# Last mode group summed in PSUM and copied in halves: one change to a fused attention and spectral-mix kernel

## The chip, the core and the metric

The kernel runs on one core of one Trainium2 chip. The metric is the device time of one execution in microseconds (us); the kernel before took 444.08 us in the median of 3 runs (444.06 to 444.13). Engines are called as in the profile: PE is TensorE (PEld its weight loads), DVE is VectorE, ACT is ScalarE, POOL is GpSimd, SP is SyncE, whose queue issues DMAs.

## What is computed

A linear attention with exponential features (batch 8, 8 heads, 576 positions, head size 64) gives x of shape 8 x 576 x 512. Then a spectral mix follows, cut here to what matters:

```
X = rfft(x, axis=1)[:, :64]                    # 64 modes
Yr = X.real @ w_r[m] - X.imag @ w_i[m]         # per mode m, 512 x 512 weights
Yi = X.real @ w_i[m] + X.imag @ w_r[m]
y = irfft(Y, n=576)                            # 64 modes, the rest zero
u = x + y
out = u + maximum(u @ w_ch, 0)                 # w_ch is 512 x 512
```

The mode weights w_r and w_i are the bulk of what is read: 64 x 512 x 512 float32 each. The DMA casts them to bf16.

## The kernel before

**Stages.** The first stage (attention, forward transform, and the early groups of the mode products) ends near 315 us. The second stage works off the remaining mode groups as their weights arrive. The last stage computes the output in 18 units. Inside `tc.manual_schedule()` each engine runs its instructions in the order of the program text, so a place in the text is a place in every engine's queue.

**Mode groups.** There are 32 groups (`groups`). The weights of a group are two tiles, `wr` and `wi`, of 128 x 8 x 512 bf16, each filled by two DMAs of POOL's queue. From group 8 on, a group covers 8 modes and 128 of the 512 input channels, and the passes over the channels add up in `Yacc` (float32, SBUF). `mode_mm` (L415) does the products of a group, 8 with `wr` and 8 with `wi`, each with 32 stationary columns and 512 moving ones, into one PSUM bank `psY`. `mode_sum` (L448) adds `psY` to `Yacc`. In the last pass it writes a bf16 tile `yst` instead (L469); for the last group, 31, in two halves of 256 columns. Group 30's sum goes to `zy7[:, 1]`.

**From a group's sum to Z and Y.** `transposed` (L852) transposes the sum on PE (L855) and copies it to `sY` (L856). From `sY` come Z, its product with w_ch (`whole_z`, L772, for groups 30 and 31), and Y regrouped by batch. They go to `zy` (`zall` and `yall`): one slot per batch, the modes on the partitions. Batch 0 has slot 8, all others their own number.

**x W.** In the waiting time, PE also does x times w_ch ahead: `flip_x` (L696) transposes two tiles of x, and `times_w` (L707) multiplies them in 8 products into two `psW` banks, each copied to `xw` by ACT (L714).

**Output units.** Unit n adds, in PSUM, x W (`add_xw`, L793) and the inverse transform of Z (`add_z`, L801) in `psB`; ACT takes the relu (L806). x (`add_x`, L808) and the inverse transform of Y (`spec`, L815) go to `psA`; DVE adds the relu to it (L820). Eight of the 18 units are "late": they skip `add_x`, and POOL adds x afterwards (L823). SP issues the output DMAs (L953). Even units use the PSUM bank pairs T0 (`psB`) and T1 (`psA`) of the pool `psumA`; odd units use T2 and T3, which lie in a pool that is opened at n = 1, when `psumL` (tags `tr`, `pW` with two banks, `pY`) is closed. So unit 1's `psB` waits until all of `psumL` is free.

**The order at the seam** (L905 to L937). After group 30: one `times_w`; the `wr` half of group 31; the last `times_w`, with ACT's copy of group 30's Z (`z7`, in T1) to `zy7` between its two `xw` copies; two SP DMAs of `zy7` to `zy`; `add_xw` of unit 0; the `wi` half of group 31 (which waits for the last weights); `add_x` of unit 0; the sum in two halves by DVE, each sent to `yall` by a DMA; transposes, copies, Z of group 31 (L925), its rows of Y (`psR`, L927), the copies to slot 8 (L929, L930), the copy `st` of the whole Z (L932), and DMAs from `st` to the other slots. Then the units start.

Of the kernel before, what the change touches and what calls it, by code (L numbers as in the profile page):

```python
# [26 lines left out]
def kernel(  # L27
# [420 lines left out]
    def mode_sum(k, psY, pb=None):  # L448
        g, gi = groups[k]
        if gi < 0:  # L450
            G = -1 - gi
            if g == 0:
                nc.vector.tensor_copy(Yacc[:, 2 * G:2 * G + 2, :], psY)  # L453
            else:
                nc.vector.tensor_tensor(
                    out=Yacc[:, 2 * G:2 * G + 2, :], in0=psY, in1=Yacc[:, 2 * G:2 * G + 2, :],
                    op=ALU.add)
        elif g < 3:
            nc.vector.tensor_tensor(
                out=Yacc[:, gi, :], in0=psY, in1=Yacc[:, gi, :], op=ALU.add)  # L460
        else:

            cuts = [0, DMODEL] if k < 31 else [0, DMODEL // 2, DMODEL]
            yst = []
            for a, b in zip(cuts, cuts[1:]):
                t = zy7[:, 1] if k == 30 else pb.tile(
                    [128, b - a], BF16, name="yst", tag="yst" if k < 31 else f"yst{a}",
                    bufs=2 if k < 31 else 1)
                nc.vector.tensor_tensor(out=t, in0=psY[:, a:b], in1=Yacc[:, gi, a:b], op=ALU.add)  # L469
                yst += [t[:, x:x + 128] for x in range(0, b - a, 128)]  # L470
                Yst.append((t, gi, a, b))
            return yst

# [203 lines left out]
    psumA = ctx.enter_context(tc.tile_pool(name="psumA", bufs=1, space=bass.MemoryType.PSUM))  # L679
    psum_cm = tc.tile_pool(name="psumL", bufs=1, space=bass.MemoryType.PSUM)  # L680
    psum = psum_cm.__enter__()

    zy = pb.tile([128, B_ + 1, 2, DMODEL], BF16, name="zy", bufs=1)
    zall, yall = zy[:, :, 0], zy[:, :, 1]
    zy7 = pb.tile([128, 2, DMODEL], BF16, name="zy7", bufs=1)
    Yst = []
    xw = pb.tile([128, B_ * NCH - N_EARLY, DMODEL], BF16, name="xw", bufs=1)

    todo = list(range(N_EARLY, B_ * NCH, 2))
# [3 lines left out]
    def slot(b):  # L693
        return b or B_
# [12 lines left out]
    def times_w(between=None):  # L707
        i, sT = ahead.pop(0)
        for x in range(2):
            ps = psum.tile([128, DMODEL], F32, name="psW", tag="pW", bufs=2)  # L710
            for dc in range(4):
                nc.tensor.matmul(ps, lhsT=sT[:, x, dc, :], rhs=wchb[:, dc, :],  # L712
                                 start=(dc == 0), stop=(dc == 3))
            nc.scalar.copy(xw[:, i + x - N_EARLY, :], ps)  # L714
            if x == 0 and between:
                between()
# [73 lines left out]
    def cuts(u):  # L790
        return (slice(0, 1), slice(1, 2)) if u["cut"] else (slice(0, 2),)

    def add_xw(u):  # L793
        u["psB"] = ps = u["pool"]().tile([128, 2, DMODEL], F32, name="psB", tag=u["tags"][0])
        for r, x, b, c, idn, ci in parts(u):
            i = b * NCH + c
            nc.tensor.matmul(ps[r, x, :], lhsT=idn,  # L797
                             rhs=xw0[:, i, :] if i < N_EARLY else xw[:, i - N_EARLY, :],
                             start=True, stop=False)

# [5 lines left out]
            nc.scalar.activation(u["o"][:, s, :], ps[:, s, :], ACT.Relu)  # L806

    def add_x(u):  # L808
        u["psA"] = ps = u["pool"]().tile([128, 2, DMODEL], F32, name="psA", tag=u["tags"][1])
        if not u["late"]:  # L810
            for r, x, b, c, idn, ci in parts(u):
                nc.tensor.matmul(ps[r, x, :], lhsT=idn, rhs=xs_all[:, b * NCH + c, :],
                                 start=True, stop=False)
# [13 lines left out]
    for n, (b, c, late) in enumerate(seq):  # L827
        u = dict(b=b, c=c, late=late == 1, half=c == 4, cut=n in (0, 17), n=n,
                 tags=("T0", "T1") if n % 2 == 0 else ("T2", "T3"),
                 pool=(lambda: psumA) if n % 2 == 0 else (lambda: psum))  # L830
        units.append(u)

    def output_tile(u):
# [15 lines left out]
                        ap=[[9 * DMODEL, 64], [5 * DMODEL, 2], [1, m * DMODEL]]),  # L849
                o[:, s, :].rearrange("p c e -> p (c e)")))  # L850

    def transposed(yst, sY, gi, pts, ident):  # L852
        for (a, b), pt in pts:
            for dc in range(a, b):
                nc.tensor.transpose(pt[:, dc - a, :], yst[dc], ident)  # L855
            nc.vector.tensor_copy(sY[:, a:b, gi % 2, :], pt)  # L856

    def modes_of(k, part, psY=None):
        if part == 0:
            while issue["k"] < min(k + NW, 32):  # L860
                weights(issue["k"])
                issue["k"] += 1
            issue_weights()
        return mode_mm(k, "pY", (part,), psY)

    def piece():
        times_w()
# [1 line left out]
            flip_x()  # L869

    ident_q = pb.tile([128, 128], BF16, name="ident_q", bufs=1)
    issue = dict(k=k_in)
    pieces_behind = (22, 24, 26, 28, 30)
    with tc.manual_schedule():
        flip_x()
        flip_x()
        nc.vector.tensor_copy(ident_q.rearrange("r (y x c) -> r c x y", x=2, y=4),
                              ident_b.rearrange("r (c x y) -> r c x y", x=2, y=4))
        for k in range(k_out, 31):
            gi = groups[k][1]  # L880
            psY = modes_of(k, 0)
            piece()
            regroup(99)
            modes_of(k, 1, psY)
            yst = mode_sum(k, psY, pb)
            if k in pieces_behind:
                times_w()
            if yst is not None:
                if gi % 2 == 0:
                    sY = pb.tile([128, 4, 2, 128], BF16, name="sY", tag="sY")  # L890
                transposed(yst, sY, gi, (((0, 4), psum.tile([128, 4, 128], BF16, name="ptY",
                                                            tag="tr")),), ident_b)
            if k in pieces_behind and todo:
                flip_x()
            if yst is not None and gi % 2 == 1 and k < 30:
                by_batch(sY, gi // 2)
                regroup(2)
            else:
                if k == 30:
                    z7 = psumA.tile([128, 2, DMODEL], F32, name="psZ", tag="T1")[:, 0]  # L900
                    whole_z(z7, 1)
                for tag in ("T1", "T0"):
                    if reorder:
                        reordered(tag)
        assert not todo and not copies and not reorder  # L905
        times_w()
        psY = modes_of(31, 0)
        times_w(lambda: nc.scalar.copy(zy7[:, 0], z7))
        assert not ahead
        nc.sync.dma_start(zy[112:128, slot(0)], zy7[0::8])  # L910
        nc.sync.dma_start(zy[112:128, 0:B_], zy7)
        u0 = units[0]
        add_xw(u0)
        modes_of(31, 1, psY)
        add_x(u0)
        yst = mode_sum(31, psY, pb)
        rows = slice(96, 112)
        for (t, _, a, b), eng in zip(Yst[-2:], (nc.sync, nc.gpsimd)):
            eng.dma_start(yall[rows, 0:B_, a:b], t)
        transposed(yst, sY, 6, [  # L920
            (dcs, psum.tile([128, 2, 128], BF16, name="ptY", tag=tag, bufs=bufs))
            for dcs, tag, bufs in (((0, 2), "tr", 1), ((2, 4), "pW", 2))], ident_q)
        r = psum.tile([16, DMODEL], F32, name="psR", tag="tr")
        z = psum.tile([128, DMODEL], F32, name="psZ", tag="pW", bufs=2)
        whole_z(z, 0)  # L925
        for dc in range(4):
            nc.tensor.matmul(r[:, dc * 128:(dc + 1) * 128], lhsT=sY[:, dc, 0, 0:16],  # L927
                             rhs=ident_b, start=True, stop=True)
        nc.scalar.copy(zall[rows, slot(0), :], z[0:16])  # L929
        nc.vector.tensor_copy(yall[rows, slot(0), :], r)  # L930
        st = pb.tile([128, DMODEL], BF16, name="st", bufs=1)
        nc.scalar.copy(st, z)  # L932
        nc.vector.tensor_copy(zall[rows, 1, :], st[32:48])
        for b, eng in ((2, nc.gpsimd), (3, nc.sync), (4, nc.gpsimd),
                       (5, nc.sync), (6, nc.gpsimd), (7, nc.gpsimd)):
            a = 16 * (b % 4 * 2 + b // 4)
            eng.dma_start(zall[rows, b, :], st[a:a + 16])  # L937

        for n, u in enumerate(units):
            if n == 1:  # L940
                psum_cm.__exit__(None, None, None)
                psum = ctx.enter_context(
                    tc.tile_pool(name="psumT", bufs=1, space=bass.MemoryType.PSUM))
            output_tile(u)
            if n:
                add_xw(u)
            add_z(u)
            if n:
                add_x(u)
            spec(u)  # L950
            while leave and leave[0] <= n:
                for dst, part in units[leave.pop(0)]["dmas"]:
                    nc.sync.dma_start(dst, part)  # L953
# [30 lines left out]
```

## Time and profile before

| what | us |
|---|---|
| median of 3 timed runs | 444.08 |
| the profiled execution's own time | 442.89 |
| its span, first to last instruction | 441.1 |
| PE busy, of the span | 313.3 |
| DVE busy | 292.6 |
| ACT busy | 280.1 |
| last mode products (L440) start | 404.89 |
| first product of `add_z` (L804) starts | 408.48 |
| last sum of the output (L820) ends | 437.25 |

The page of the profile gives busy times by engine, the span in 40 slices, and the chain of work that ended last. A timeline lists instructions by start, merged where the same ones follow each other; the number in brackets is the idle time ahead of an instruction and what ended it. Durations of matmuls include their latency: products of 512 columns start every 0.215 us, and each shows 0.379 us. A few matmul records are missing from the trace, so that a group of 8 can show as x7.

### The profile page before, as it was taken

What the parts mean: (1) busy time and instruction counts of PE and PEld (TensorE: products, weight loads), DVE (VectorE), ACT (ScalarE), POOL (GpSimd) and SP (SyncE); (2) the same over time, 40 slices, a digit from 0 to 9 for tenths busy, and PEclk for the clock granted to TensorE, in tenths of its full rate; (3) what the DMA queues carried; (4) which work ended last, traced back from release to release, by engine and by line L of the source; (5) the groups of instructions that cost most, each with busy time, mean ns of one, the idle gap of its engine ahead of it and who ended that gap; (6) DMA issues with size and microseconds to landing.
All of it is one profiled execution on the core that took longest, in us unless ns stands there. A gap on an engine that the chain in (4) does not pass through costs nothing.

```text
span 441.1 us, 10731 instructions
## 1 busy us (share of the span) xinstructions
PE 313.3 (71%) x4391; PEld 197.0 (45%) x4409; DVE 292.6 (66%) x422; ACT 280.1 (63%) x623; POOL 212.0 (48%) x301
## 2 busy tenths in 40 slices
PE   1777578776665877687654777667698667678995
PEld 0465455554554654465332544434344334343442
DVE  4778889989888778678835786654223354462884
ACT  3776688887787787678723886663264254343763
POOL 6775448585557666446525464443142222200780
PEclk9999999999999699779957888988899898989998
DMA  8999999999999999999999999999999999996498
GB/s 188 249 227 217 218 230 219 230 219 217 227 224 222 222 234 219 223 230 225 221 222 222 222 221 211 211 211 211 211 211 211 211 211 211 211 211 114 142 402 330
DMA packets 61057, 97.81 MB, mean 222 GB/s; under 512 B 3921, under 2 KB 28849, under 8 KB 61009
## 3 DMA queue, kind: packets, MB, share of 16 engines
q0 software_dynamic: 51952, 76.62, 96.4%
q1 hardware_dynamic: 8896, 20.45, 13.3%
q8 instruction: 34, 0.56, 0.5%
q10 hardware_dynamic: 160, 0.07, 0.1%
q14 instruction: 15, 0.11, 0.1%
HBM read 163.64 MB, written 9.44 MB: 392 GB/s over the span
## 4 chain that ended last, share of the span: by engine, by line
DMA 42%; DVE 20%; PE 20%; ACT 11%; issue 4%; POOL 2%; DVEq 0%; ACTq 0%; SPq 0%; POOLq 0%
DMA wi<-in_moe_w_i_dram 26%; DVE mkq L247 8%; DMA wchb<-in_moe_w_ch_dram 4%; DMA wr<-in_moe_w_r_dram 4%; DMA k<-in_k_dram 4%; ACT AA L258 3%; ACT AA L254 3%; PE psY L440 2%; DVE nd L336 2%; DVE tB L329 2%; DVE xs_all L350 2%; PE psB L804 2%; PE psB L797 2%; PE psA L818 2%; DMA kn<-in_k_dram 2%
## 5 line engine op out<-in xcount | busy, mean ns | idle before, releaser
L284 POOL TENSOR_TENSOR vaug<-vn,ee 128x576 bf16<-128x576 f32 x64 | 73.2, 1161 | 59.2 <-ACT ee L269 55.4
L254 ACT ACTIVATE AA<-psT 128x1024 bf16<-128x1024 f32 x64 | 62.0, 1021 | 27.5 <-PE psT L222 26.8
L170 POOL DMA_DIRECT2D wr<-in_moe_w_r_dram x48 | 29.7, 621 | 68.4 <-PE psY L440 27.8
L258 ACT ACTIVATE AA<-psk 128x1024 bf16<-128x1024 f32 x64 | 61.4, 1010 | 0.0
L276 ACT ACTIVATE e<-mkq 64x4 f32<-64x4 f32 (+1 forms) x128 | 26.3, 206 | 48.1 <-DVE mkq L247 45.7
L170 POOL DMA_DIRECT2D wi<-in_moe_w_i_dram x48 | 30.0, 626 | 44.1 <-DMA wi<-in_moe_w_i_dram 12.9
L247 DVE TENSOR_REDUCE mkq<-psk 128x8 f32<-128x1024 f32 x32 | 38.8, 1213 | 2.9 <-PE psk L213 2.8
L247 DVE TENSOR_REDUCE mkq<-psq 128x8 f32<-128x1024 f32 x32 | 39.0, 1220 | 1.6 <-PE psq L213 1.5
L440 PE MATMUL psY<-wi,XT 128*32 128x512 bf16 x192 | 18.1, 451 | 25.4 <-DMA wi<-in_moe_w_i_dram 25.4
L329 DVE TENSOR_TENSOR tB<-psNB,e 128x650 f32<-128x650 f32 x32 | 26.6, 832 | 13.0 <-PE psNB L319 12.7
L714 ACT CAST xw<-psW 128x512 bf16<-128x512 f32 x34 | 19.9, 587 | 22.7 <-PE psW L712 20.0
L440 PEld LDWEIGHTS <-XT 128*32 128x32 bf16 x384 | 14.9, 172 | 43.0 <-DMA wi<-in_moe_w_i_dram 19.9
L712 PE MATMUL psW<-wchb,sT 128*128 128x512 bf16 x128 | 33.2, 393 | 0.6 <-issue 0.2
L319 PEld LDWEIGHTS <-AA 128*128 128x128 bf16 x640 | 26.4, 104 | 12.4 <-issue 12.3
L704 DVE COPY sT<-pt 128x1024 bf16<-128x1024 bf16 x17 | 11.8, 692 | 29.4 <-PE pt L701 26.8
L200 PE MATMUL ptr<-ident_b,k 128*128 128x128 bf16 x160 | 16.1, 238 | 21.2 <-DVE qT L206 19.2
L206 DVE COPY kT<-ptr 128x640 bf16<-128x640 bf16 x32 | 15.7, 492 | 21.3 <-PE ptr L200 21.3
L336 DVE TENSOR_TENSOR nd<-psNA,tB 128x650 f32<-128x650 f32 x32 | 26.7, 835 | 3.3
L350 DVE TENSOR_TENSOR xs_all<-nd,rden 128x640 bf16<-128x640 f32 x32 | 27.2, 851 | 1.1
L300 PE MATMUL kvz<-vaug,AA 64*128 64x65 bf16 x1152 | 26.4, 199 | 1.0 <-DVE Yacc L453 0.6
L385 ACT CAST XT<-psx 64x128 bf16<-64x128 f32 x96 | 24.9, 260 | 2.9 <-PE psx L377 1.9
L222 PE MATMUL psT<-qT,w 64*128 64x512 bf16 x64 | 13.9, 424 | 16.9 <-DVE mkq L247 16.9
(151 smaller groups left out, 734.2 us busy)
## 6 DMA issues: line engine op xcount, KB each, us to landing
wr<-in_moe_w_r_dram POOLq DMA_DIRECT2D x62, 512.0 KB, 18.7
wi<-in_moe_w_i_dram POOLq DMA_DIRECT2D x62, 512.0 KB, 18.3
out_dram<-of SPq DMA_DIRECT2D x14, 512.0 KB, 3.5
vn<-in_v_dram SPq DMA_DIRECT2D x24, 288.0 KB, 6.1
q<-in_q_dram POOLq DMA_DIRECT2D x12, 288.0 KB, 16.3
k<-in_k_dram POOLq DMA_DIRECT2D x12, 288.0 KB, 17.1
vn<-in_v_dram SPq DMA_DIRECT2D x16, 144.0 KB, 6.4
Yacc<-in_moe_w_r_dram POOLq DMA_DIRECT2D x2, 512.0 KB, 9.1
```

The source lines that it names most:

```text
L170: nc.gpsimd.dma_start(t.rearrange("p (m i) e -> p m (i e)", i=2), w[8 * gi + y:8 * gi + 8:2, g * 128:(g + 1) * 128, :].rearrange("m (p i) ...
L247: nc.vector.tensor_reduce(out=o, in_=i, axis=AX.X, op=ALU.max, apply_absolute_value=True)
L254: nc.scalar.activation(AA[:, 0, ab, 0:1024].rearrange("f (x j p) -> f j x p", j=2, p=64), st["psT"].rearrange("f j (x p) -> f j x p", p=64 ...
L258: nc.scalar.activation(AA[:, 1, ab, 0:1024].rearrange("p (c j f) -> p c j f", c=4, j=2), st["psk"], ACT.Exp, scale=sc)
L284: nc.gpsimd.tensor_tensor(out=vaug[:, ab, :, 0:64], in0=st["v"], in1=ee[:, ab, :].unsqueeze(2).to_broadcast([128, 9, D_]), op=ALU.mult,)
L300: nc.tensor.matmul(kvz[:, hh, ab * 65:(ab + 1) * 65], lhsT=AA[r, 1, ab, 128 * j:128 * j + 128], rhs=vaug[r, ab, j, :], start=(j == 0), sto ...
L319: nc.tensor.matmul(p[:, hh, 65 * c:65 * c + 65], lhsT=AA[:, 0, ab, x:x + 128], rhs=kvzF[:, hh, ab * 65:(ab + 1) * 65], start=True, stop=True,)
L329: nc.vector.tensor_tensor(out=tB, in0=st["psNB"], in1=e2.unsqueeze(3).to_broadcast([128, 2, NCH, 65]), op=ALU.mult,)
L336: nc.vector.tensor_tensor(out=nd, in0=st["psNA"], in1=st["tB"], op=ALU.add)
L350: nc.vector.tensor_tensor(out=xo, in0=nd[:, :, :, 0:64], in1=rden.to_broadcast([128, 2, NCH, 64]), op=ALU.mult,)
L440: nc.tensor.matmul(psY[32 * j:32 * j + 32, :], lhsT=XT[:, 16 + 32 * ri:48 + 32 * ri, 32 * i + 4 * gi + j], rhs=wt[ri][:, 2 * j + i, :], st ...
L712: nc.tensor.matmul(ps, lhsT=sT[:, x, dc, :], rhs=wchb[:, dc, :], start=(dc == 0), stop=(dc == 3))
```

## The change

Four things change at the seam.

- Group 31 has no DVE addition any more. Its accumulator goes into PSUM first, as a float32 product of an identity (`ident_f2`, new) with `Yacc`, in two halves of 256 columns in two banks (`seeds`, tags `pY` and `tr`). The mode products add to it in two halves (`last_mm`: 32 products of 256 columns for 16 of 512). ACT copies half 0 to `yst`, DVE half 1.
- The transposed halves are copied by the two engines (half 0 by DVE, half 1 by ACT). Z and the rows of Y are computed in halves of 256 output columns, one bank each, and `zall`, `yall` and `st` are copied in halves: half 0 by ACT, half 1 by DVE. The rows of Y come straight from `yst` through columns of the identity, not from `sY`.
- `psW` gets a pool of its own, `psumW`. It is closed after the last `times_w`, and unit 1's `psB` (T2) lies in its banks, so that `add_xw` of unit 1 runs ahead of the units: one of its two products before the last mode products, one behind them. T3 lies in the banks of `psumL` as before.
- The order: group 30's second `times_w` stands ahead of group 30's `wi` products; ACT's copy of `z7` stands behind both `xw` copies of the last `times_w`; `add_x` of unit 0 stands ahead of group 31's `wi` products.

The core of the diff:

```diff
+    def add_xw(u, xs=(0, 1)):
+        if 0 in xs:
+            u["psB"] = u["pools"][0]().tile([128, 2, DMODEL], F32, name="psB", tag=u["tags"][0])
...
-                 pool=(lambda: psumA) if n % 2 == 0 else (lambda: psum))
+                 pools=(lambda: psumA,) * 2 if n % 2 == 0 else (lambda: psumW, lambda: psum))
...
+    def seeds():
+        ps = []
+        for h, tag, e, _ in halves:
+            p = psum.tile([128, 256], F32, name="psL", tag=tag)
+            nc.tensor.matmul(p, lhsT=ident_f2, rhs=Yacc[:, groups[31][1], e], start=True, stop=False)
+            ps.append(p)
+        return ps
+
+    def last_mm(ps, ri):
+        g, gi = groups[31]
+        for h, _, e, _ in halves:
+            for i in range(2):
+                for j in range(4):
+                    nc.tensor.matmul(
+                        ps[h][32 * j:32 * j + 32, :],
+                        lhsT=XTs[g % 2][:, 16 + 32 * ri:48 + 32 * ri, 32 * i + 4 * gi + j],
+                        rhs=W[31][ri][:, 2 * j + i, e],
+                        start=False, stop=(i == 1 and ri == 1),
+                    )
...
             piece()
+            if k == 30:
+                times_w()
             regroup(99)
             modes_of(k, 1, psY)
             yst = mode_sum(k, psY, pb)
-            if k in pieces_behind:
+            if k in pieces_behind and k < 30:
                 times_w()
...
         times_w()
-        psY = modes_of(31, 0)
-        times_w(lambda: nc.scalar.copy(zy7[:, 0], z7))
+        psL = seeds()
+        modes_of(31, 0)
+        last_mm(psL, 0)
+        times_w()
         assert not ahead
+        psumW_cm.__exit__(None, None, None)
...
+        nc.scalar.copy(zy7[:, 0], z7)
         nc.sync.dma_start(zy[112:128, slot(0)], zy7[0::8])
         nc.sync.dma_start(zy[112:128, 0:B_], zy7)
-        u0 = units[0]
+        u0, u1 = units[0:2]
         add_xw(u0)
-        modes_of(31, 1, psY)
+        add_xw(u1, (0,))
         add_x(u0)
-        yst = mode_sum(31, psY, pb)
+        last_mm(psL, 1)
         rows = slice(96, 112)
...
+        for (h, _, e, copy), eng in zip(halves, (nc.sync, nc.gpsimd)):
+            t = pb.tile([128, 256], BF16, name="ystL", tag=f"yst{h}", bufs=1)
+            copy(t, psL[h])
+            eng.dma_start(yall[rows, 0:B_, e], t)
+            yst.append(t)
+        add_xw(u1, (1,))
+        for h, tag, e, copy in halves:
+            pt = psum.tile([128, 2, 128], BF16, name="ptY", tag=tag)
+            for x in range(2):
+                nc.tensor.transpose(pt[:, x, :], yst[h][:, 128 * x:128 * x + 128], ident_q)
+            ptY.append(pt)
+        for (h, *_), copy in zip(halves, (nc.vector.tensor_copy, nc.scalar.copy)):
+            copy(sY[:, 2 * h:2 * h + 2, 0, :], ptY[h])
+        zr = []
+        for h, tag, e, _ in halves:
+            p = psum.tile([128, 2, 256], F32, name="psZ", tag=tag)
+            nc.tensor.matmul(p[0:16, 1, :], lhsT=ident_b[:, 0::8], rhs=yst[h], start=True, stop=True)
+            zr.append(p)
+        for h, _, e, _ in halves:
+            for dc in range(4):
+                nc.tensor.matmul(zr[h][:, 0, :], lhsT=sY[:, dc, 0, :], rhs=wchb[:, dc, e],
+                                 start=(dc == 0), stop=(dc == 3))
         st = pb.tile([128, DMODEL], BF16, name="st", bufs=1)
-        nc.scalar.copy(st, z)
+        for dst, src, x in ((zall[rows, slot(0)], slice(0, 16), 0),
+                            (yall[rows, slot(0)], slice(0, 16), 1), (st, slice(0, 128), 0)):
+            for h, _, e, copy in halves:
+                copy(dst[:, e], zr[h][src, x, :])
```

More of the change, by code (lines that the diff above doesn't have):

```diff
@@ L461, in mode_sum @@
         else:
[L463 to L472, printed above, removed]
+            t = zy7[:, 1] if k == 30 else pb.tile([128, DMODEL], BF16, name="yst", tag="yst")
+            nc.vector.tensor_tensor(out=t, in0=psY, in1=Yacc[:, gi, :], op=ALU.add)
+            return [t[:, x:x + 128] for x in range(0, DMODEL, 128)]
     def zeros(i):
@@ L681 @@
     psum = psum_cm.__enter__()
+    psumW_cm = tc.tile_pool(name="psumW", bufs=2, space=bass.MemoryType.PSUM, side="right")
+    psumW = psumW_cm.__enter__()
     zy = pb.tile([128, B_ + 1, 2, DMODEL], BF16, name="zy", bufs=1)
@@ L685 @@
     zy7 = pb.tile([128, 2, DMODEL], BF16, name="zy7", bufs=1)
-    Yst = []
     xw = pb.tile([128, B_ * NCH - N_EARLY, DMODEL], BF16, name="xw", bufs=1)
@@ L709, in times_w @@
         for x in range(2):
-            ps = psum.tile([128, DMODEL], F32, name="psW", tag="pW", bufs=2)
+            ps = psumW.tile([128, DMODEL], F32, name="psW", tag="pW")
             for dc in range(4):
@@ L791, in cuts @@
         return (slice(0, 1), slice(1, 2)) if u["cut"] else (slice(0, 2),)
-    def add_xw(u):
-        u["psB"] = ps = u["pool"]().tile([128, 2, DMODEL], F32, name="psB", tag=u["tags"][0])
+    def add_xw(u, xs=(0, 1)):
+        if 0 in xs:
+            u["psB"] = u["pools"][0]().tile([128, 2, DMODEL], F32, name="psB", tag=u["tags"][0])
         for r, x, b, c, idn, ci in parts(u):
+            if x not in xs:
+                continue
             i = b * NCH + c
-            nc.tensor.matmul(ps[r, x, :], lhsT=idn,
+            nc.tensor.matmul(u["psB"][r, x, :], lhsT=idn,
                              rhs=xw0[:, i, :] if i < N_EARLY else xw[:, i - N_EARLY, :],
@@ L808, in add_x @@
     def add_x(u):
-        u["psA"] = ps = u["pool"]().tile([128, 2, DMODEL], F32, name="psA", tag=u["tags"][1])
+        u["psA"] = ps = u["pools"][1]().tile([128, 2, DMODEL], F32, name="psA", tag=u["tags"][1])
         if not u["late"]:
@@ L850, in output_tile, with transposed @@
                 o[:, s, :].rearrange("p c e -> p (c e)")))
[L852 to L856, printed above, removed]
+    def transposed(yst, sY, gi):
+        pt = psum.tile([128, 4, 128], BF16, name="ptY", tag="tr")
+        for dc in range(4):
+            nc.tensor.transpose(pt[:, dc, :], yst[dc], ident_b)
+        nc.vector.tensor_copy(sY[:, :, gi % 2, :], pt)
+    halves = [(h, tag, slice(256 * h, 256 * h + 256), eng) for h, tag, eng in
+              ((0, "pY", nc.scalar.copy), (1, "tr", nc.vector.tensor_copy))]
+    def seeds():
[16 more added lines that the diff above has]
+                    )
     def modes_of(k, part, psY=None):
@@ L863, in modes_of @@
             issue_weights()
-        return mode_mm(k, "pY", (part,), psY)
+        return mode_mm(k, "pY", (part,), psY) if k < 31 else None
     def piece():
@@ L871 @@
     ident_q = pb.tile([128, 128], BF16, name="ident_q", bufs=1)
+    ident_f2 = pb.tile([128, 128], F32, name="ident_f2", bufs=1)
     issue = dict(k=k_in)
@@ L878 @@
                               ident_b.rearrange("r (c x y) -> r c x y", x=2, y=4))
+        nc.vector.tensor_copy(ident_f2, ident_b)
         for k in range(k_out, 31):
@@ L890 @@
                     sY = pb.tile([128, 4, 2, 128], BF16, name="sY", tag="sY")
-                transposed(yst, sY, gi, (((0, 4), psum.tile([128, 4, 128], BF16, name="ptY",
-                                                            tag="tr")),), ident_b)
+                transposed(yst, sY, gi)
             if k in pieces_behind and todo:
@@ L906 @@
         times_w()
-        psY = modes_of(31, 0)
-        times_w(lambda: nc.scalar.copy(zy7[:, 0], z7))
+        psL = seeds()
+        modes_of(31, 0)
+        last_mm(psL, 0)
+        times_w()
         assert not ahead
+        psumW_cm.__exit__(None, None, None)
+        psumW = ctx.enter_context(
+            tc.tile_pool(name="psumT", bufs=1, space=bass.MemoryType.PSUM, side="right"))
+        nc.scalar.copy(zy7[:, 0], z7)
         nc.sync.dma_start(zy[112:128, slot(0)], zy7[0::8])
         nc.sync.dma_start(zy[112:128, 0:B_], zy7)
-        u0 = units[0]
+        u0, u1 = units[0:2]
@@ L913 @@
         add_xw(u0)
-        modes_of(31, 1, psY)
+        add_xw(u1, (0,))
         add_x(u0)
-        yst = mode_sum(31, psY, pb)
+        last_mm(psL, 1)
         rows = slice(96, 112)
[L918 to L930, printed above, removed]
+        yst, ptY = [], []
+        for (h, _, e, copy), eng in zip(halves, (nc.sync, nc.gpsimd)):
[3 more added lines that the diff above has]
+            yst.append(t)
@@ L931 @@
+        for h, _, e, _ in halves:
+            for dc in range(4):
+                nc.tensor.matmul(zr[h][:, 0, :], lhsT=sY[:, dc, 0, :], rhs=wchb[:, dc, e],
+                                 start=(dc == 0), stop=(dc == 3))
         st = pb.tile([128, DMODEL], BF16, name="st", bufs=1)
-        nc.scalar.copy(st, z)
+        for dst, src, x in ((zall[rows, slot(0)], slice(0, 16), 0),
+                            (yall[rows, slot(0)], slice(0, 16), 1), (st, slice(0, 128), 0)):
+            for h, _, e, copy in halves:
+                copy(dst[:, e], zr[h][src, x, :])
@@ L942 @@
                 psum = ctx.enter_context(
-                    tc.tile_pool(name="psumT", bufs=1, space=bass.MemoryType.PSUM))
+                    tc.tile_pool(name="psumU", bufs=1, space=bass.MemoryType.PSUM))
             output_tile(u)
-            if n:
+            if n > 1:
                 add_xw(u)
```

## The prediction

> **What bounds the kernel now.** I read the page first. DMA is at nine tenths in the 40 slices until about 400 us, and the TensorE row only nears ten tenths in the last five slices. So the kernel has a long stage that waits for the weight stream and a short last stage that computes the output. The change touches the seam between the two. The chain of waits, cut to that seam, comes next (start us, us, what):
>
> ```profile
> 384.38 20.46 DMA wi<-in_moe_w_i_dram
> 404.85 0.04 issue
> 404.89 0.68 PE psY L440 x7
> 405.57 0.54 PE psA L812 x2
> 406.11 0.29 PE ptY L855 x2
> ...
> 406.43 0.30 DVE sY L856
> ...
> 406.78 1.05 PE psZ L772 x4
> ...
> 407.85 0.58 ACT zy L929
> ...
> 408.48 0.59 PE psB L804 x2
> ```
>
> The last imaginary weights land at 404.85. From there to the first output product at 408.48 it is 3.59 us from hand to hand: mode products, sum, transpose, copy, Z, copy. I call 404.89 **T** (start of the last mode products) and 408.48 **S** (first `add_z`). L812 stands in the chain only because PE runs in order; what its time covers is VectorE's sum (L469, 405.62 to 406.38 in the timeline). After S the chain names PE with hardly a gap until 435.87. Then comes the last sum, two output DMAs (256 KB, 2.5 and 2.6 us to land) and the end of the span at 441.1.
>
> The second view is the timeline of PE and then of ACT just ahead of T (start, us, engine line op ... [idle before <- releaser]):
>
> ```profile
> 401.39 0.69 PE L440 MATMUL psY<-wr,XT 128*32 128x512 bf16 x8
> 402.01 1.90 PE L712 MATMUL psW<-wchb,sT 128*128 128x512 bf16 x8
> 403.75 0.59 PE L797 MATMUL psB<-xw,ident_p 128*128 128x512 bf16 x2
> 404.89 0.68 PE L440 MATMUL psY<-wi,XT 128*32 128x512 bf16 x8 [0.55 <-DMA wi<-in_moe_w_i_dram]
> ```
>
> ```profile
> 403.09 0.59 ACT L714 CAST xw<-psW 128x512 bf16<-128x512 f32 x1 [1.00 <-PE psW L712]
> 403.57 0.59 ACT L908 CAST zy<-psZ 128x512 bf16<-128x512 f32 x1
> 404.05 0.60 ACT L714 CAST xw<-psW 128x512 bf16<-128x512 f32 x1
> ```
>
> PE has only 0.55 us to spare ahead of the weights. ACT copies z7 between the two xw copies; it has left the bank pair T1 by 404.16, well before L812 writes there at 405.50.
>
> **Work ahead of T.** Moving `times_w` at group 30 fills the 1.69 us in which PE waited for group 30's weights (idle before L440 at 395.03): 8 products, 1.74 us by L712's starts (402.01 to 403.75), so those mode products slip only from 395.03 to about 395.1. Without the product group in between, transposes, copy, flip and z7's Z follow at once: 0.71 us to the sum, 0.69 sum, then 0.44, 0.48 and 0.44 as in the rows of before, so L772 starts near 397.95 and not at 398.71. That needs T1 free of ACT's two L757 copies. They are queued behind two more xw copies now: last product out near 395.26, xw to 395.9, two copies of 1.01 to 397.85. It just fits. The seeds then start near 400.63 (before, the next PE work was at 401.39).
>
> Seeds: two float32 products of 256 columns. The only float32 row on PE is (ns of one, min/median/max; first and last start):
>
> ```profile
> L554 PE MATMUL pct<-ident_f,trig x5: 327/328/328, 100.8 to 134.2; 128*128 128x128 f32 x5
> ```
>
> At 109.20 and 134.21 the next matmul started 0.17 us after it, so 128 columns cost at most 0.17 us of PE and 256 cost 0.34; two are 0.7 us. Bounds: 0.2 (bf16, half of L797's 0.43 spacing for two of 512) and 1.05 (four of the slowest spacing, 0.26, seen at 100.76). I take 0.7, the nearest row. [...]
>
> The first half of the last mode products is 16 products of 256 columns where 8 of 512 were: 0.62 us as at 401.39, since the columns are the same. So the last `times_w` runs from 401.93 to 403.67, within 0.1 us of before: what moved earlier pays for the seeds.
>
> **The new wait.** `add_x(u0)` (0.43 us) now stands ahead of the last mode products on PE, and it writes T1, where z7 sits. z7's copy moved behind both xw copies on ACT. The second product group is out 0.20 us after its last start slot (381.64 to 381.84 at group 29), 403.87; xw to 404.46; z7 starts 0.48 after xw (as 403.57 to 404.05), ends 404.94; PE gets `add_x` at 405.00 and is through at 405.43. Behind that instruction on PE waits everything: the last mode products first. So T goes from 404.89 to about 405.45, **+0.56**, though the weights are there at 404.85. `add_xw(u1)` in the freed psW banks waits for xw at 404.5 and is covered. Bounds: 0 (z7 early enough) and 1.0 (seeds at the upper bound, T1 freed 0.1 late). SP's two zy7 DMAs move with z7 by 0.8 us; the larger took 4.5 us to land, so 410.2, and the unit that reads it first (n=2) needs it near 411.3. The two yst DMAs land near 410.6 by their 3.7 and 3.2 us; n=2 needs them near 411.7. Covered by about 1 us.
>
> **The chain from T, by halves.** ACT at 128x256 from float32 PSUM: 0.39 us (the copy group L394, 128x256). DVE at 256: 0.42 (L469). Handoffs 0.02 to 0.06 as in the chain above.
>
> - half 0 products out at T+0.50 (8 starts of 33 ns, as L440's 8 last started 0.31 after the first with one 0.21 round between; then 0.11 for 256 columns and 0.17 of latency, 0.38 less 0.21); half 1 at T+0.77.
> - ACT's copy to T+0.93, DVE's (half 1) to T+1.21. Before, VectorE's second half ended at T+1.49.
> - transposes 0.29: half 0 by T+1.28, DVE copy 0.29 to T+1.58; half 1 by T+1.56, ACT copy to T+1.97. Before: 2.16.
> - row products on PE wait for that ACT copy through their bank; Z starts at T+2.15. Each half is 4 products of 256, 0.43, plus latency: out at T+2.74 and T+3.17. Before, Z began at T+1.89 with the half of sY that was there; now both halves of Z need all of sY.
> - ACT copies Z half 0 by T+3.14, DVE half 1 by T+3.60 (0.41); `add_z` at T+3.66.
>
> So S lies 3.66 behind T where it lay 3.59: **+0.07**. 0.2 us gained up to sY is lost where Z no longer overlaps its copy and the last copy is VectorE's. Bounds 3.3 (every new copy 0.1 cheaper) and 4.1. The yall copies end at T+3.92, `spec(u0)` asks for them at T+4.09.
>
> **The output stage.** Two psB products of u1 leave it, 0.43 us of PE. But its first units run close to other engines (ACT, then DVE):
>
> ```profile
> 410.45 1.02 ACT L806 ACTIVATE of<-psB 128x1024 f32<-128x1024 f32 x1 [0.26 <-ACT of L806]
> 411.69 1.02 ACT L806 ACTIVATE of<-psB 128x1024 f32<-128x1024 f32 x1 [0.22 <-DMA zy<-st]
> ```
>
> ```profile
> 411.50 5.06 DVE L820 TENSOR_TENSOR of<-psA,of 128x1024 f32<-128x1024 f32 x4 [0.48 <-ACT of L806]
> ```
>
> u0's two relus end at S+1.71, so u1's relu can come at S+1.73 and not at S+1.54; before it was at S+1.97. VectorE's sum of u1 then ends at S+4.00, and u3, which needs that bank, gets it at S+4.05 where PE would be there at S+3.91; before, S+4.31. From there on all is 0.26 us earlier: **-0.26**. Bounds 0 and -0.43. The last output DMAs took 2.5 and 2.6 us where the first 256 KB took 2.7, so no queue of transfers stands at the end; PE's end moves the kernel's.
>
> **Sum:** 0.56 + 0.07 - 0.26 = +0.37. The span of 441.1 would be 441.5. The profiled execution took 442.89, of which 1.79 lie around the span; the median of the timed runs is 444.08, 1.19 above it. I add the difference to the median: 444.45, said as **444.5**.
>
> **Rivals.** 0.2% is 0.9 us, about what a measurement of this kernel can tell from no change.
>
> - *Forecast* (0.60): z7's copy sets T. 444.1 to 444.9.
> - *The weights still set T, or the halves are quicker than counted* (0.22). Then -0.2 with T at 404.89; with 3.3 us from T to S, -0.55; with the whole 0.43 out of the output, -0.7: 443.4 to 443.9. For it: PE's two xw halves and z7 all sit within 0.6 us of the weights. Against it: the order of the three copies on ACT is written out, and T1 has one buffer. A share of 0.04 goes past -0.9.
> - *More handoffs than I see* (0.10): T1 freed late at 397.9 shifts seeds, `times_w`, xw and z7 alike, seeds at 1.05, S at T+4.1, no gain in the output: 0.91 + 0.51 = +1.4 at most, 445.5; half of it past +0.9.
> - *The clock drops* (0.08), the one that is clearly slower. Windows of 3.41 us (us, then busy PE, PEld, DVE, ACT, POOL; granted clock, DMA share, GB/s):
>
> ```profile
> 383.59:387.00 3.41, 1.54 (x20) 0.85 (x24) 1.12 (x2) 0.00 (x0) 0.61 (x1) 1.00 1.12 211
> 387.00:390.41 3.41, 3.41 (x60) 1.95 (x56) 1.80 (x2) 0.00 (x0) 0.00 (x0) 0.50 1.12 211
> 404.07:407.48 3.41, 2.76 (x20) 0.91 (x18) 1.34 (x4) 0.58 (x2) 0.37 (x1) 1.00 0.44 93
> ```
>
> A stretch with PE busy for 1.54 us was followed by one at half clock; one with 2.76 was not. The finer chain has more holes for PE. If its stretch fell to about 1.5, the next 3.41 us would run at 0.50 and PE would lose 1.7 us: 446.2. Against it: I count some 3.0 us busy there, as the work moved ahead of T fills the gap of before. [...]
>
> **Range:** 443.6 to 445.4; it leaves out the clock's case and the far ends of the two middle ones, some 0.15. Faster by over 0.2%: 0.04. Within: 0.83. Slower: 0.13 (0.08 and half of 0.10).
>
> **What would show it.** z7's copy after both xw copies, ending near 404.9, and L812's successor on PE waiting for ACT and not for the wi DMA; last mode products at about 405.45; first `add_z` 3.66 later; last `spec` about 27.1 us after that where it was 27.4. A wait of the last mode products for the DMA would make the first term wrong; a granted clock of 0.5 after 404 would make the whole sum wrong; a seed pair over 1 us moves T by the excess.

## The result, and the profile after

The changed kernel takes 445.08 us in the median of 22 runs (443.09 to 447.61); the kernel before, on the same chips, 444.01 us (22 runs, 442.41 to 445.48). The ratio is 1.0033 with a 95% interval of 1.002 to 1.0045: slower by 0.9 to 2.0 us, where I had forecast 0.4 us and "within 0.2%" as by far the likeliest.

The profiled execution took 446.37 us with a span of 444.6. It is one of the slower ones: the two spans differ by 3.5 us, the medians by 1.07. So I do not compare the spans; I cut both at marks that mean the same in each. *Landing* is when the last wi transfer lands (POOL's last issue plus its time to landing, 386.65 + 19.6 here), **T** the start of the last mode products, **S** the first `add_z`, *last sum* the end of DVE's last output sum. Landings and ends are read from rounded figures and are good to 0.05 us (the chain of before puts its landing at 404.85).

| us | before | after |
|---|---|---|
| landing of the last weights | 404.88 | 406.25 |
| landing to T | 0.01 | 0.66 |
| T to S | 3.59 | 3.73 |
| S to the last sum | 28.77 | 28.42 |
| last sum to the end of the span | 3.85 | 5.54 |

The weights landed 1.37 us later in this execution, which has nothing to do with the seam (see the last section). The other four rows add up to +2.1 us: +0.65, +0.14, -0.35 and +1.69.

The chain of waits at the seam of the changed kernel (start us, us, what), which answers to the chain of before:

```profile
405.27 0.59 ACT xw L708
405.85 0.50 ACT zy L938
...
406.39 0.59 PE psA L809 x2
406.98 0.43 PE psL L871 x8
407.44 0.38 ACT ystL L950
...
407.87 0.57 PE ptY L957 x4
408.46 0.38 ACT sY L960
...
408.88 0.27 PE psZ L964
409.15 0.99 PE psZ L968 x8
...
410.17 0.43 DVE zy L974
...
410.64 0.60 PE psB L801 x2
```

The DMA is no longer what the last mode products (L871) wait for: the chain runs through ACT's two last copies and `add_x(u0)` (L809). The timeline of ACT shows the three copies in their new order:

```profile
404.40 0.59 ACT L708 CAST xw<-psW 128x512 bf16<-128x512 f32 x1 [1.86 <-PE psW L706]
405.27 0.59 ACT L708 CAST xw<-psW 128x512 bf16<-128x512 f32 x1 [0.28 <-PE psW L706]
405.75 0.59 ACT L938 CAST zy<-psZ 128x512 bf16<-128x512 f32 x1
```

z7's copy ends at 406.34, L809 starts at 406.39. The fourth row of the table is a surprise. The views of the queue of SP give it; first SP's own waits near the end, before and after (engine line <- whom: us in total, times, longest):

```profile
SPq L979 <- DMA out_dram<-of: 1.3, 2, 0.6
```

```profile
SPq L1021 <- DMA out_dram<-of: 2.3, 2, 1.8
```

and the DMA view of the changed kernel for 436 to 443 us (40 slices of 0.175 us; then queues with packets, MB, share; then issues with the median time to landing):

```profile
GB/s 421 515 328 445 398 374 375 421 468 374 398 398 328 398 293 386 421 410 363 374 363 363 375 386 456 351 375 351 374 293 0 12 12 23 23 23 23 23 23 12
...
q8 instruction: 1, 0.02, 0.8%
...
out_dram<-of SPq DMA_DIRECT2D x2, 256.0 KB, 4.3
```

All DMA engines stop at 441.2 but one, which goes on alone at 23 GB/s until 442.9 (a sixteenth of the 388 GB/s that the 16 engines move together before, in 418 to 439.6 us, is 24). And there is a packet of another queue: 16 KB of *instructions*, at 440.4 us by the trace's DMA records, 0.88 us long. In the kernel before, in 418 to 439.6 us, there is no such packet, and all DMA engines end together:

```profile
DMA  5999999999999999999999997999999999999996
...
q1 hardware_dynamic: 2704, 8.39, 98.6%
...
out_dram<-of SPq DMA_DIRECT2D x2, 256.0 KB, 2.6
```

This line says something that I had not weighed: from 418 us on, all 16 DMA engines are full with output. The landing times that I did read (2.5 and 2.6 us) are as short as the 2.7 us of the first 256 KB, though the engines are 98.6% busy; by my reading, because they run out together.

### The profile page after: what moved, and what is told of

It is laid out like the page before. It is cut to its first block, busy times and chain, and to the rows that moved or that the text cites. A ratio compares the mean times of both kernels' runs of the same rounds, so it can differ in the third digit from the quotient of the medians.

```text
span 444.6 us, 10783 instructions
## 1 busy us (share of the span) xinstructions
PE 321.3 (72%) x4412; PEld 203.4 (46%) x4431; DVE 292.5 (66%) x423; ACT 280.8 (63%) x626; POOL 212.1 (48%) x301
## 4 chain that ended last, share of the span: by engine, by line
DMA 32%; DVE 24%; PE 23%; ACT 13%; issue 5%; POOL 1%; DVEq 0%; ACTq 0%; SPq 0%; POOLq 0%
DMA wi<-in_moe_w_i_dram 18%; DVE mkq L247 9%; DMA wr<-in_moe_w_r_dram 8%; ACT AA L254 4%; DMA k<-in_k_dram 4%; DVE nd L336 3%; DVE tB L329 3%; PE psW L706 3%; ACT AA L258 3%; DVE xs_all L350 3%; PE psY L440 2%; ACT e L276 2%; PE psx L367 2%; PE psB L801 2%; PE psA L815 2%
## 5 line engine op out<-in xcount | busy, mean ns | idle before, releaser
L319 PEld LDWEIGHTS <-AA 128*128 128x128 bf16 x640 | 28.2, 108 | 11.9 <-issue 11.7
L200 PE MATMUL ptr<-ident_b,k 128*128 128x128 bf16 x160 | 17.1, 249 | 21.0 <-DVE qT L206 19.4
L440 PE MATMUL psY<-wi,XT 128*32 128x512 bf16 x184 | 16.9, 442 | 20.9 <-DMA wi<-in_moe_w_i_dram 20.9
L213 PE MATMUL psk<-w,kT 128*128 128x256 bf16 x128 | 23.2, 313 | 2.0 <-ACT xw L413 0.9
```

Source lines behind the costliest of these rows:

```text
L319: nc.tensor.matmul(p[:, hh, 65 * c:65 * c + 65], lhsT=AA[:, 0, ab, x:x + 128], rhs=kvzF[:, hh, ab * 65:(ab + 1) * 65], start=True, stop=True,)
L440: nc.tensor.matmul(psY[32 * j:32 * j + 32, :], lhsT=XT[:, 16 + 32 * ri:48 + 32 * ri, 32 * i + 4 * gi + j], rhs=wt[ri][:, 2 * j + i, :], st ...
```

## The experiments

Theory 1, formed from these lines: PE's code is fetched by DMA, 16 KB at a time. In the records of this queue the packets follow each other in steps of some 250 PE rows (matmuls and weight loads): 250 in the mean of the last 20 steps of after_again and of after_look3, 228 to 285 among the last five. Before has 34 packets, the last at 413.9 us. The change adds 37 rows to PE's program by my count in the two programs (8815 to 8852; the traces record 44 more, 8818 and 8862, with before's missing records put back), and the next packet slips in ahead of the end. In the seven profiles that have a 35th packet and no gaps, PE had started 8841 to 8862 rows when it came, so for the changed kernel that is right at the end of its program. Rivals: chance (such a packet comes now and then, whatever the kernel), and the order of copies at the seam as the only cause.

**before_48more.** The kernel before, with 48 PE rows nobody needs, far from the output.

```diff
             regroup(99)
+            if k in (21, 23, 25, 27):
+                idle = psum.tile([128, 6, 32], F32, name="idle", tag="tr")
+                for i in range(6):
+                    nc.tensor.matmul(idle[:, i, :], lhsT=ident_b, rhs=ident_b[:, 0:32],
+                                     start=True, stop=True)
             modes_of(k, 1, psY)
```

> The kernel before with 24 small products (32 columns, into a bank that nobody reads; 48 PE rows with their weight loads) in the waiting time of groups 21, 23, 25 and 27, which have nothing to do with the output. Theory 1: the last code packet comes at the end as in the changed kernel, the last sum's end to the span's end takes 5.5 us in the place of 3.85, the kernel is 1 to 1.7 us slower than before. Theory 2, and the theory that only the new order at the seam counts: 3.9 us there, time within 0.3 us of before.

It was 1.0014 of before (0.9992 to 1.0036; medians 444.45 and 443.63). The time alone can't settle it; the profile does. T lies within 0.1 of the landing, S and the last sum are those of before (3.58, 28.78), and from the last sum to the end it takes 5.27 us. Its DMA view for 434 to 442:

```profile
GB/s 369 410 430 471 348 410 348 451 328 451 389 287 430 307 400 410 358 430 369 369 420 369 348 430 369 358 420 164 20 31 20 31 20 31 20 0 0 0 0 0
...
q8 instruction: 1, 0.02, 0.7%
...
out_dram<-of SPq DMA_DIRECT2D x2, 256.0 KB, 4.0
```

The same picture in a kernel whose seam is untouched: the packet (at 434.7), one engine left alone, landings of 4.0 us.

**before_130more** and **before_240more**: 65 and 120 such products, in groups 25 to 29 (`range(13)` and `range(24)` for `range(6)`). They shift the packet along the output stage.

> The kernel before with 65 small products nobody reads (130 PE rows) in the waiting time of groups 25 to 29. If the place of the code packet among the output DMAs decides, the last packet now comes some 8 to 12 us ahead of the end, well inside the stretch in which all 16 DMA engines are full (418 to 440 us of before): 5.3 us from the last sum to the end in this profile, and as a packet so far inside is there in every execution, 1.4 us slower than before in the mean (with 48 rows more it was 0.6). If what counts is the order at the seam only: 3.9 us and no change.

> The same with 120 products (240 PE rows). If the place of the packet decides, it now comes ahead of the full stretch or at its start (near 415 us), its engine has time to catch up, and the last sum's end to the span's end is 3.9 us again: as fast as before (within 0.5 us), though it has the most PE rows. If added rows cost time as such, it is slower than with 130.

Measured: 1.0018 (1.0001 to 1.0035; medians 444.63 and 443.61) with 130 rows, 1.0005 (0.9986 to 1.0024; 443.6 and 443.61) with 240. Views of 428 to 442 of the first; of 416 to 418 and of 437 to 442 of the second:

```profile
q8 instruction: 1, 0.02, 0.4%
...
out_dram<-of SPq DMA_DIRECT2D x2, 256.0 KB, 3.5
```

```profile
q8 instruction: 1, 0.02, 3.8%
```

```profile
out_dram<-of SPq DMA_DIRECT2D x2, 256.0 KB, 2.6
```

At 428.4 us the packet costs 0.9 us at the end (4.76, expected 5.3), at 416.8 nothing (3.89), though that kernel has the most rows. Rows are not what costs; where the packet falls is. The times agree in sign, but their intervals are as wide as the effect. That the packet costs less at 428.4 than at 434.7 would fit an engine that catches up on part of the delay; no run separates this. Nor does any show why the delay of 1.4 to 1.7 us is longer than the packet's own 0.88.

**after_again, after_look3, after_look4, after_look5**: the changed kernel four times more, for its profile, and **before_look2**, the kernel before.

> The changed kernel once more, for a second profile of it. Theory 1 (a late code packet): PE's code comes in packets of 16 KB, one per some 250 PE rows; the 37 rows that the change adds bring one more at the very end, and the output packets behind it on its DMA engine land late. It then stands in this profile too, within 2 us of the last output DMA, which lands 4 us after its issue and not 2.6; from the last sum's end to the span's end it is 5.5 us, not 3.85. Theory 2 (chance): no such packet at the end, 3.9 us. In both the last mode products start 0.6 us behind the last weights (z7's copy), and 3.7 us lie from there to the first add_z. Time: the kernel before + 1.1 us in the mean.

> The changed kernel, a third profile: how often does its last code packet fall among the output DMAs (2 of 2 so far, at 440.4 and 435.2 us; none in two other kernels with the same number of PE rows)? If always: 5.3 us or more from the last sum to the end. If now and then: 3.85 is to be seen in some profile of it. T 0.66 behind the weights, or more if the clock was at half during group 29's batches.

> The changed kernel, a fourth profile: 5.3 us from the last sum to the end where the 35th packet comes before some 441 us, 3.85 where it comes later. T 0.66 to 1.0 behind the last weights with a full clock during group 29's batches, over 1.3 with half.

> The changed kernel, a fifth profile, with the same two questions as the fourth: where the 35th packet of code comes against the last output DMAs, and whether T's lateness goes with the clock during group 29's batches.

> The kernel before, a second profile. With 8815 rows its last code packet should lie near 414 us and none at the end: 3.85 us from the last sum to the end, T within 0.1 us of the last weights whatever the clock does during group 29.

after_again, which was timed, gave 1.0031 (1.0018 to 1.0044; medians 444.93 and 443.63). The table has all profiles of the two kernels (us; the packet's time in its trace):

| profile | landing | to T | T to S | S to last sum | to the end | last code packet |
|---|---|---|---|---|---|---|
| before | 404.88 | 0.01 | 3.59 | 28.77 | 3.85 | 413.9 |
| before_look2 | 406.35 | 0.68 | 3.59 | 28.77 | 3.81 | 416.0 |
| after | 406.25 | 0.66 | 3.73 | 28.42 | 5.54 | 440.4 |
| after_again | 405.07 | 0.69 | 3.73 | 28.41 | 5.30 | 435.2 |
| after_look3 | 404.77 | 0.98 | 3.73 | 28.41 | 3.81 | 442.9, behind the last output packet |
| after_look4 | 405.88 | 1.78 | 3.73 | 28.42 | 3.89 | 445.9, behind the span |
| after_look5 | 405.86 | 0.68 | 3.73 | 28.41 | 3.82 | 414.0, no 35th in the trace |

So the packet falls among the output DMAs in two of five executions, and in both the end is 1.4 to 1.7 us later. The changed kernel's 22 times would fit that (11 lie between 443.1 and 444.8, 11 between 445.3 and 447.6), but do not show it: the nine times of after_again have no such gap, and the landing alone differs by 1.5 us between executions. In after_look3 nothing is left to fetch among the output of 436 to 441:

```profile
out_dram<-of SPq DMA_DIRECT2D x2, 256.0 KB, 2.5
```

The table ends with the span, and the packet may cost something behind it. An execution's own time is 1.8 us above its span in both looks at the kernel before, in after, in after_again and in all eight variants with another number of rows than the changed kernel's. In after_look3, after_look5, after_z7mid and after_order it is 1.9 to 2.0 above, and in after_look4 3.0 (446.72 for a span of 443.7). There the packet came 2.3 us behind the last instruction; the DMA view of 443 to 446.5 us has nothing else:

```profile
q8 instruction: 1, 0.02, 1.8%
```

What the execution's end waited for in after_look4 is not shown; that the 1.2 us more are the packet's is my guess.

The expectation for before_look2, T at the weights whatever the clock does, failed: 0.68. The clock was at half from 397.9 to 401.3 us there, and the 8 products of a `times_w` took 2.82 us by the timeline where they took 1.90. In the first look PE stood idle for 0.55 us ahead of T; the kernel before has no more slack than that.

**after_48fewer**: the changed kernel with 48 PE rows less. The columns of `sY` are put in order by a permuted identity, so that the first pair's rows of Y take 8 products of 128 columns in the place of 32 products of 32.

```diff
-                nc.tensor.matmul(
-                    ps[32 * j:32 * j + 32, dc * 128:(dc + 1) * 128],
-                    lhsT=cols[dc][:, j + 4 * h::8], rhs=ident_b, start=True, stop=True)
+            cols = by_hand(sY)[:, dc, h].rearrange("p j g c -> p (j g c)")
...
+            for r in ([slice(0, 128)] if (P, zr) in merged else
+                      [slice(32 * j, 32 * j + 32) for j in range(4)]):
+                nc.tensor.matmul(out[r], lhsT=cols[:, r], rhs=rhs, start=start, stop=stop)
```

> The changed kernel with 48 PE rows less: batches' rows of Y of the first pair of groups by 8 products of 128 columns in the place of 32 of 32 (the columns of sY are put in the needed order by the transposition). Theory 1: no code packet at the end, 3.9 us from the last sum to the end; the kernel is 1 to 1.7 us faster than the changed one and stands at before + 0.4 us (T + 0.6, chain + 0.1, output - 0.35). Theory 2: as the changed kernel.

The end is as expected, 3.85 us, no packet later than 416.5. The time is not: 1.0025 (1.0011 to 1.004), 444.78 against 443.63. In its profile T lies **1.74** behind the landing (the clock was at half from 387.4 to 390.8 us in it). That opened the second question: what holds PE ahead of T?

**after_z7mid** and **after_order**: z7's copy back between the two xw copies; in after_order both products of `add_xw(u1)` also move behind the last mode products.

```diff
-        times_w()
+        times_w(lambda: nc.scalar.copy(zy7[:, 0], z7))
...
-        add_xw(u1, (0,))
         add_x(u0)
         last_mm(psL, 1)
```

> The changed kernel with ACT's copy of z7 back between the two xw copies of the last x W product. My forecast's first term: the last mode products then wait for the second half of add_xw(u1) or for the weights and not for z7; they start 0.0 to 0.2 us behind the landing in the place of 0.66, and the kernel is 0.5 us faster than the changed one. The rival (something else holds PE there): still 0.6 us behind. The end stays as in the changed kernel (5.5 us behind the last sum by theory 1), as PE's rows are the same number.

> The changed kernel with z7's copy between the two xw copies and both products of add_xw(u1) behind the last mode products (in the holes of the chain), rows of PE as in the changed kernel. The last mode products should start within 0.15 us of the last weights' landing in the place of 0.66, the chain to the first add_z 3.7 to 3.9 us, the output stage as in the changed kernel (28.4 us to the last sum). End as in the changed kernel (5.4 or 3.9 us, as the packet falls). Time: 0.5 us under the changed kernel. If PE's products ahead of the weights are too many (the seeds measured 0.96 us for the pair), it starts later than 0.3 us behind them.

after_z7mid: 1.0018 (1.0006 to 1.003; 444.27 and 443.63), T still 0.52 behind the landing. My expectation was wrong: three copies end when they end, and the last one now is xw's, on which `add_xw(u1)` waits through the freed bank, as PE's timeline of this kernel has it:

```profile
405.39 0.38 PE L794 MATMUL psB<-xw,ident_p 128*128 128x512 bf16 x1 [0.36 <-ACT xw L708]
405.60 0.59 PE L809 MATMUL psA<-xs_all,ident_p 128*128 128x512 bf16 x2
406.12 0.69 PE L871 MATMUL psL<-wi,XT 128*32 128x256 bf16 x16
```

after_order takes that wait away too, and the DMA is back as the releaser, with T 0.03 behind the landing:

```profile
405.19 0.59 PE L809 MATMUL psA<-xs_all,ident_p 128*128 128x512 bf16 x2
405.94 0.69 PE L871 MATMUL psL<-wi,XT 128*32 128x256 bf16 x16 [0.15 <-DMA wi<-in_moe_w_i_dram]
```

Its time: 1.0018 (0.9999 to 1.0036; 444.25 and 443.61). So the wait is shown, and its price is 0.6 us in the profile; the times can't resolve it.

**after_240more, after_fix, after_order_240more**: combinations. The first is the changed kernel with the 120 idle products; after_fix is after_order with 48 rows less and Z ahead of the rows of Y; the last is after_order with Z first and the idle products.

> The changed kernel with the 120 small products (240 PE rows) in the waits of groups 25 to 29. Theory, in its three parts: the code packet comes ahead of the full stretch (near 412), so 3.85 us from the last sum to the end; PE's clock stays at full speed through the products of group 29's batches, so that group 30's wi products start at the landing and T lies 0.66 behind the last weights and not 1.4 to 1.7; the rest as in the changed kernel (3.73 and 28.42). Sum against before: +0.66 + 0.14 - 0.35 = +0.45 us; 0.7 us under the changed kernel in the mean. If the packet and the clock are not what adds to my forecast, it is as slow as the changed kernel (+1.1 us or more).

> As after_order, and with 48 PE rows less (the first batches' rows of Y by 8 products for 32), and Z ahead of the rows of Y, so that Z's first products run while ACT still copies sY's second half. Start within 0.15 us of the weights, 3.4 us from there to the first add_z (3.73 in the changed kernel), 28.4 us to the last sum, 3.85 us to the end: 1.3 to 1.8 us under the changed kernel in its executions with the late packet, and 0.3 to 0.6 us under the kernel before.

> The same with z7's copy between the xw copies, both products of add_xw(u1) behind the last mode products, and Z ahead of the rows of Y. T within 0.1 us of the last weights, 3.65 us to the first add_z, 28.42 to the last sum, 3.85 to the end: 0.3 us under the kernel before in these parts, 0.7 us under after_240more. Time: before - 0.3 us, with an uncertainty of 0.5.

Measured: 1.0055 (1.0035 to 1.0074; 446.12 and 444.05), 1.0007 (0.9987 to 1.0028; 443.81 and 443.61) and 1.0002 (0.9984 to 1.002; 444.21 and 444.05). All three end 3.80 to 3.91 us after the last sum: no packet in the full stretch. But T lies 3.09, 1.37 and 2.28 us behind the landing, so the forecast of T failed in all three. Of the times, that of after_240more (+0.45 us expected) is clearly off; the other two expectations lie within the intervals. I had expected the idle products of the first and the last to keep PE's clock up; they did not. The stretches of after_240more and, for comparison, of after_again (us, busy PE, PEld, DVE, ACT, POOL; granted clock, DMA share, GB/s):

```profile
388.00:391.40 3.40, 2.33 (x20) 1.05 (x24) 0.93 (x2) 0.00 (x0) 0.00 (x0) 0.50 1.12 211
391.40:395.00 3.60, 3.60 (x61) 1.81 (x54) 2.88 (x3) 0.77 (x1) 0.00 (x0) 0.56 1.12 211
```

```profile
388.00:391.40 3.40, 3.19 (x75) 2.05 (x68) 2.37 (x2) 1.26 (x2) 0.00 (x0) 1.00 1.12 211
391.40:395.00 3.60, 3.57 (x23) 1.76 (x22) 3.21 (x4) 2.49 (x4) 0.00 (x0) 1.00 1.12 211
```

With the clock at half while PE works off group 29's batches, group 30's wi products started at 398.81 in after_240more, 2.5 us behind the landing of their weights; in after_again it was 395.17, right at the landing. In all five profiles of the changed kernel T follows these products by 10.57 to 10.60 us. In the kernel before it was 9.86 with the weights as the end of it, and 1.69 us of waiting ahead of group 30's wi products took up a slow stretch (387.0 to 390.4 at half clock there, and T on time):

```profile
395.03 0.67 PE L440 MATMUL psY<-wi,XT 128*32 128x512 bf16 x8 [1.69 <-DMA wi<-in_moe_w_i_dram]
```

The change has put `times_w` into that wait. after_look4 is the changed kernel's own case: clock 0.62 in 388 to 391.4, no wait left ahead of these products, which start 1.1 us behind the landing of their weights (395.94), and T 1.78 late:

```profile
388.00:391.40 3.40, 2.96 (x44) 1.70 (x48) 1.22 (x2) 0.00 (x0) 0.00 (x0) 0.62 1.11 209
```

```profile
397.06 0.69 PE L440 MATMUL psY<-wi,XT 128*32 128x512 bf16 x8
```

All 17 profiles fit. With the order of before, three had a half clock between 384 and 392 us, and group 30's wi products still started at the landing. With the order of the changed kernel six had one between 385 and 395; in five of them these products started 1.1 to 2.5 us late, and in after_z7mid just in time.

**before_u1**: one part of the change alone, unit 1's `add_xw` ahead in the psW banks, on the kernel before.

```diff
+        add_xw(units[1])
         nc.scalar.copy(zall[rows, slot(0), :], z[0:16])
...
-            if n:
+            if n > 1:
                 add_xw(u)
```

> One part of the change alone on the kernel before: psW in banks of its own, both products of unit 1's add_xw ahead of the units (on PE behind the rows of Y, while ACT copies Z); no seeds, no halves, the order of z7 and add_x(u0) as before. The same number of PE rows as before, so no late code packet. T within 0.1 us of the last weights, 3.6 us to the first add_z, 28.42 us to the last sum in the place of 28.77, 3.85 to the end: 0.35 us under the kernel before, which the times can hardly tell. If the packet of code or the clock ahead of T were no part of the changed kernel's loss, this would have to show a loss too.

Its ratio is 0.9995 (0.9975 to 1.0015; 443.63 and 443.89). S to the last sum is 28.40 and the end 3.84, as expected; T was 1.04 late in this execution, with the clock at half from 396.1 to 399.5. A half clock behind group 30's wi products goes with a late T in the order of before as well, here and in before_look2. The gain of 0.37 us stands in the profile and is too small for the times. No version beat the kernel before beyond its interval.

## Why the prediction was wrong, step by step

That 445.08 lies inside the range of 443.6 to 445.4 was luck: the upper end stood for more handoffs at the seam, and the larger part of the excess lies in things that the sum did not have.

- **Work ahead of T.** Right in kind: `times_w` filled the wait, T1 came free in time, the last `times_w` (403.33, 6.99 us behind group 30's wi products) stood close to its forecast place (401.93 against 395.1, 6.8). The seeds were mis-sized: 0.96 us for the pair (401.75 to 402.71), where I had 0.7. The row of the changed kernel has four matmuls where I counted two:

```profile
L862 PE MATMUL psL<-Yacc,ident_f x4: 379/379/379, 401.8 to 402.4; 128*128 128x256 f32 x4
```

  The four start 0.22 us apart, and the next products start 0.31 us behind the last of them (402.40 to 402.71). The 0.17 us of a float32 transpose of 128 columns, from which I took the 0.7, was too small a measure.
- **The new wait at T1.** Right: +0.66 measured, +0.56 forecast, and the releaser is the one named. `add_xw(u1)`, which I had called covered, was so only behind z7's copy: in after_z7mid its wait for the last xw copy held PE instead. after_order took both away.
- **The chain by halves.** +0.14 where I had +0.07. Z first (after_fix, after_order_240more) gets 0.08 back, 3.65; I had expected 0.3 of it.
- **The output stage.** -0.35 where I had -0.26. ACT's three relus run without a hole (411.29, 2.00 us for three), each starting 0.10 us before the one ahead has ended by its record; so unit 1's starts 1.62 behind S, 0.11 earlier than I allowed.
- **The failed step:** "no queue of transfers stands at the end; PE's end moves the kernel's". The 16 DMA engines are full from 418 us on; the page that I had read says so in its last two slices (DMA in tenths, 11 us each):

```profile
DMA  8999999999999999999999999999999999996498
```

  And the cost of the change in *rows of PE's program* was nowhere in the sum. Where the changed kernel's 35th code packet falls into that stretch, the end is 1.4 to 1.7 us later.
- **A cover counted as free.** Filling the wait of 1.69 us ahead of group 30's wi products cost nothing in the profile that I read, but in that profile the wait had taken up a half clock from 387.0 to 390.4: in after_look4 T came 1.1 us later for it. I had set the clock as a rival at the wrong place, behind T.

Put together for the five profiles of the changed kernel: T is 0.96 us late on average, the end 0.64 us later than 3.83, with +0.14 and -0.35: +1.4 us against a kernel that is always on time at T, +1.05 against the mean of the two looks at the kernel before (0.35 late). What the five have around the span, 0.3 us more in the mean, makes it some +1.3. The measured interval is 0.9 to 2.0. Five profiles are few, one of them gives all but a little of that 0.3, and the shares of the causes are not better known than to a factor of two.

Open is why the packet comes at 435, at 443 or not at all in executions of one and the same program. after_z7mid and after_order, with the same 8852 rows, had no 35th packet in their one profile each. The boundary lies within PE's last instructions, and no view shows when the fetch is asked for.

## What to carry to other kernels

Where the last stage fills all DMA engines, count the instructions that a change adds, not only their time: here code came through the same engines, and with a packet among the last transfers one of them went on alone and the end came 5.3 to 5.5 us behind the last sum, not 3.8 to 3.9. A wait on an engine is not spare room only because it is off the chain in one profile; look at what it absorbs in other profiles of the same kernel, such as one with the clock at half. And moving a copy to the end of a queue moves everyone who needs its bank: list who writes that bank next.

## What the runs showed of the hardware

- The packets of the instruction queue, by theory 1 PE's code: 16 KB each, one per some 250 PE rows (228 to 285 late in the traces), 0.88 to 1.30 us long in before and after. With one at 440.4, 435.2 or 434.7 us the span's end came 1.4 to 1.7 us later, at 428.4 0.9, at 416.8 and earlier not at all.
- A float32 product of 256 columns that is no transpose took two matmuls, started 0.22 us apart, with weight loads of 0.19 us.
- The landing of the last weights differs between executions (404.77 to 406.35 in the table), in both kernels. Two with late landings, after and before_look2, had the clock at half for 13.7 us at 309; POOL's issues of weights wait for PE's mode products there (13.4 us the longest in after, 10.8 in before). That is not all of it: before_240more, with only 6.8 us at half from 315, landed at 406.6. The landing is as late in kernels with the order of before (404.85 to 406.6) as in those with that of the changed one (404.75 to 406.3).
